# A second pairwise sum on VectorE before the softmax denominators, with new pacing, priorities and end, in an attention and MLP kernel

## The chip, the cores and the metric

The kernel runs on one core of a Trainium2 chip. The metric is the device time of one launch in microseconds (us); lower is better. The profiled span is some 2 us shorter than the measured time of the same execution (1088.9 against 1091.05 us before).

## The reference, cut to what matters

```python
def reference(A_x, A_wqkv, A_wo, B_x, B_w1, B_b1, B_w2, B_b2):
    xn = _layernorm(A_x)                                   # (1, 2048, 1024)
    # A: attention, 32 heads of 32, softmax(q k / sqrt(32)) v, then @ wo
    s = _A_ref(xn, A_wqkv, A_wo)
    # B: layernorm, w1 (1024 -> 3584), tanh gelu, w2 (3584 -> 1024)
    g = _silu(_B_ref(xn, B_w1, B_b1, B_w2, B_b2))
    return A_x + s * g
```

All tensors are bf16. The outputs of the two branches meet only in the last line, so the MLP's dense matmuls can fill TensorE's time between those of attention.

## The kernel before

Attention is cut into 512 units. A unit is one group of four heads (8 groups), one block of 256 queries (8 blocks) and two blocks of 128 keys. For each unit TensorE makes scores (S), ScalarE makes two exponentials of 1024 columns, VectorE adds the two key blocks (PA), and TensorE makes P times V and the denominators, which are PA times a matrix of ones:

```python
def unit(u, pv):                                    # cut
    o = add("PE", s_fn, 2 * Q256, TL, ...)          # scores of the unit
    for h in range(2):
        x = act(... activation(P[pi]..., ACT.Exp, scale=SCALE) ...)
    pa = dve(lambda e: e.tensor_tensor(PA[ai][:], P[pi][:, :, 0, :], P[pi][:, :, 1, :], op=ALU.add), ..., 2.5)
    vc = add("PE", ...)                             # P times V: 8 matmuls
    oc = add("PE", ...)                             # ones times PA: 4 matmuls
    oc.alt = pa                                     # if pa is late, 8 matmuls on P instead
```

A planner in Python lays all operations of all engines into fixed orders before the program is built; on the chip each engine works through its own order and waits on semaphores. The planner lets a score unit go first unless "dense" work (MLP, projections, output items) is behind:

```python
if c[1] == 0 and heads["pro"] >= len(self.queues["pro"]) and \
        state["done"] < dense_total * (state["s"] - dense_slack) / total_units:
    paced = c            # the score unit is taken only if nothing else is ready
...
plan.run(HG * 64, 10)    # dense_slack = 10 units
```

An output item is eight matmuls of 512 columns (one for each head group), a gate multiply from PSUM and an add on VectorE; two items make one stored block of 128 rows. The program divides PSUM into eight banks: six hold scores, and two are shared by the dense items and the open P,V item. An eviction is the copy of a finished result out of a bank; it frees the bank.

The softmax here doesn't subtract the row's maximum and nothing guards it: scores larger than these inputs give would overflow.

Of the kernel before, what the change touches and what calls it, by code (L numbers as in the profile page):

```python
# [11 lines left out]

ENGS = ("PE", "ACT", "DVE", "POOL", "SP")
# [7 lines left out]
class _Item:  # L21
    def __init__(self, kind, due=0):
        self.kind = kind
        self.due = due
        self.chunks = []
        self.evacs = []
        self.bank = None
        self.k = 0


class _Plan:
# [3 lines left out]
    def __init__(self):  # L35
        self.ops = []
        self.last_w = {}
        self.readers = {}
        self.s_queue = []
        self.pv_queue = []  # L40
        self.queues = {"pro": [], "proj": [], "mlp": [], "wo": []}
# [36 lines left out]
    def run(self, total_units, dense_slack):  # L78
# [59 lines left out]
        def pick(e, t):  # L138
            while soon[e] and soon[e][0][0] <= t:
                _, _, o = heapq.heappop(soon[e])  # L140
                if not o.dead:
                    pend[e].append(o)
            best = None
            bk = None
            if e == "SP" and pend[e] and min(o.prio for o in pend[e]) >= 5 and state["bw"] > t + 1500:
                wake(state["bw"] - 1400, e)
                return None
            for o in pend[e]:
                k = (o.prio, o.idx)
                age = t - o.ready  # L150
                if e == "ACT" and o.prio > 0 and age > 2500:
                    k = (-1, o.idx)
                if e == "DVE" and o.prio >= 3 and age > 3500:
                    k = (1.5, o.idx)
                if bk is None or k < bk:
                    best, bk = o, k
            if best is not None and e == "DVE" and best.prio >= 2 and soon[e]:
                r = min((x[0] for x in soon[e] if x[2].prio <= 1), default=INF)
                if r < t + best.occ - 400:
                    wake(r, e)  # L160
                    return None
            if best is not None:
                pend[e].remove(best)
            return best
# [18 lines left out]
        def next_items(t):  # L183

            out = []
            u = state["s"]
            q = self.queues
            pr = q["proj"][heads["proj"]] if heads["proj"] < len(q["proj"]) else None
            if heads["pro"] < len(q["pro"]):
                out.append("pro")  # L190
            if pr is not None and u >= pr.due:
                out.append("proj")
            for n in ("mlp", "wo"):
                if heads[n] < len(q[n]):
                    out.append(n)
            if pr is not None and "proj" not in out and (u >= pr.due - 12):
                out.append("proj")
            return out

        def opens_at(it, r):  # L200

            off = 0.0
            for c in it.chunks:
                if c.left == 0:
                    r = max(r, c.ready - off)
                elif it.kind == "wo":
                    return None
                off += 1.2 * c.occ
            return r

        def pe_step(t):
# [20 lines left out]
            if state["pvopen"] is not None:  # L232
                it = state["pvopen"]
                o = it.chunks[it.k]
                if o.alt is not None and o.alt.start is None and not o.alt.dead and it.exp_of[o.unit].fin is not None \
                        and t > it.exp_of[o.unit].fin + 4000:
                    p = o.alt
                    p.dead = True
                    p.start = p.fin = t
                    if p in pend["DVE"]:  # L240
                        pend["DVE"].remove(p)
                    o.occ *= 2
                    release(p, t)
                if o.left == 0:
                    cands.append((o.ready, 1, o, None))
            if state["dopen"] is not None:
# [4 lines left out]
            else:  # L251
                bf = bank_for(t)
                if bf is not None:
# [49 lines left out]
            if opening is not None:  # L303
# [12 lines left out]
            if cls == 0:  # L316
                state["s"] += 1
            else:
                it = o.item
                it.k += 1  # L320
                if it.k == len(it.chunks):
                    if cls == 1:
                        state["pvopen"] = None
                    else:
# [6 lines left out]

        for o in self.ops:
            if o.left == 0:
# [111 lines left out]
def bass_recurrent_scan__mha_block__mixer_channel_mlp__prompt_kernel(  # L445
# [34 lines left out]
    TRIG = 7  # L480
# [3 lines left out]
    with ExitStack() as st:  # L484
# [163 lines left out]
        load_x(2)  # L648
        load_x(3)
        load_v(0)  # L650
        for t in range(4, NT):
            load_x(t)
# [163 lines left out]
        def w1_item(c, pi):  # L816
# [4 lines left out]
            it = _Item("mlp")  # L821
            for k in range(8):
# [13 lines left out]
                c_b16(512), [("xb", i3)], [("sq", p % 2)], 3)  # L836
            dve(lambda e: e.scalar_tensor_tensor(ut_t[i3][:], sq_t[p % 2][:], 1.0 / GA, xb_t[i3][:], op0=ALU.add, op1=ALU.mult),  # L837
                c_f32(512), [("sq", p % 2), ("xb", i3)], [("ut", i3)], 3)
# [4 lines left out]
                c_f32(512), [("ut", i3), ("xb", i3)], [("h", hs)], 3)  # L843
# [84 lines left out]
        def proj(hg, w):  # L928
# [9 lines left out]
            for k, (kind, t) in enumerate(lst):  # L938
                due = 64 * w + 3 + int(k * (48 if w < 6 else 26) / len(lst))
                if kind == "v":  # L940
                    plan.queues["proj"].append(v_item(hg // 2, t, "proj", due))
                else:
                    plan.queues["proj"].append(qk_item(hg, 0 if kind == "q" else 1, t, wk if kind == "k" else wq, due))

        def unit(u, pv):
# [18 lines left out]
            for h in range(2):  # L964
                x = act(lambda e, h=h: e.activation(P[pi][:, 2 * h:2 * h + 2].rearrange("p j k q -> p (j k q)"),  # L965
                                                    ps[:, pr[h] * 1024:(pr[h] + 1) * 1024], ACT.Exp, scale=SCALE),
                        c_act(1024), [("S", pr[h])], [("P", pi, h)], 0)
            pa = dve(lambda e: e.tensor_tensor(PA[ai][:], P[pi][:, :, 0, :], P[pi][:, :, 1, :], op=ALU.add), c_b16(1024),  # L968
                     [("P", pi, 0), ("P", pi, 1)], [("PA", ai)], 2.5)
# [8 lines left out]
            oc = _Op()  # L978

            def o_fn(e, b):  # L980
                if pa.dead:
                    for kk in range(2):
                        ins = quad(e, lambda j: bankp(b, j, 256, 512), lambda j: ones[:], lambda j: P[pi][:, j, kk, :],
                                   False, False)
                    return ins
                return quad(e, lambda j: bankp(b, j, 256, 512), lambda j: ones[:], lambda j: PA[ai][:, j, :], False, False)
            oc = add("PE", lambda e: o_fn(e, pv.bank), Q256, TL, [("PA", ai), ("P", pi, 0), ("P", pi, 1), ("ones",)], [], item=pv)
            oc.alt = pa
            oc.unit = u
            pv.exp_of[u] = x  # L990
            return x, vc, oc

        def norm(g, pv, ot_dst, W, extra=()):
            i = g % 2
            a = dve(lambda e: e.transpose(nt_t[i][:], bank(pv.bank, 256, 512)), c_ps(256), [], [("nt", i)], 1, pv)
            dve(lambda e: e.tensor_copy(nv_t[i][:], bank(pv.bank, 0, 256)), c_ps(256), [], [("nv", i)], 1, pv)
# [4 lines left out]
                [("nr", i)], [("nb", i)], 2.2)  # L1001
            return dve(lambda e: e.tensor_tensor(ot_dst, nv_t[i][:], nb_t[i][:], op=ALU.mult), c_f32(256),
# [3 lines left out]
        for tq in range(1, 4):  # L1006
            plan.queues["proj"].append(qk_item(0, 0, tq, wq0, 16 * tq - 12))
        for w in range(HG):
# [23 lines left out]
            for qb in range(NQB):  # L1032
# [3 lines left out]
                vcs, ocs, xs = [], [], []  # L1036
                for kp in range(NKP):
                    x, vc, oc = unit(g * 8 + kp, pv)
                    xs.append(x)
                    vcs.append(vc)  # L1040
                    ocs.append(oc)
                pv.chunks = []
                lag = 3
                for k in range(NKP + lag):
                    if k < NKP:
                        pv.chunks.append(vcs[k])
                    if k >= lag:
                        pv.chunks.append(ocs[k - lag])
# [10 lines left out]
                for t2 in range(2):  # L1059
# [10 lines left out]
                    else:  # L1070
# [3 lines left out]
                    dma(f"xr{ri}", lambda e, xr=xr, tb=tb: e.dma_start(xr, x2[tb * 128:(tb + 1) * 128, :]), 262144, [],  # L1074
                        rt + [("xr", ri, 0), ("xr", ri, 1)])
                    dma(f"gr{ri}", lambda e, gr=gr, tb=tb: e.dma_start(gr, g_d[tb * 128:(tb + 1) * 128, :]), 262144,
                        [("g_d", qb, q) for q in range(4)], rt + [("gr", ri, 0), ("gr", ri, 1)])
                    for nh in range(2):
                        it = _Item("wo")
                        for hc in range(HG):  # L1080
                            def fn(e, b, hc=hc, tb=tb, nh=nh):
                                o7 = OTr[:, hc, tb * 128:(tb + 1) * 128] if hc < 7 else ot7[:, tb * 128:(tb + 1) * 128]
                                return full(e, bank(b), o7, wo_sb[hc][:, nh * 512:(nh + 1) * 512], hc == 0, hc == HG - 1)
                            chunk(it, fn, Q512, [("OTr", hc, tb // 4) if hc < 7 else ("OT7", qb), ("wo", hc)])
                        sl_ = slice(nh * 512, (nh + 1) * 512)
                        dve(lambda e, it=it, gr=gr, sl_=sl_: e.scalar_tensor_tensor(gr[:, sl_], bank(it.bank), 0.5, gr[:, sl_],
                                                                                    op0=ALU.mult, op1=ALU.mult),
                            c_ps(512), [], [("gr", ri, nh)], 0, it)
                        dve(lambda e, xr=xr, gr=gr, sl_=sl_: e.tensor_tensor(xr[:, sl_], gr[:, sl_], xr[:, sl_], op=ALU.add),
                            c_b16(512), [("gr", ri, nh)], [("xr", ri, nh)], 1)  # L1090
                        plan.queues["wo"].append(it)
                    dma(f"os{ri}", lambda e, xr=xr, tb=tb: e.dma_start(out2[tb * 128:(tb + 1) * 128, :], xr), 262144,
                        [("xr", ri, 0), ("xr", ri, 1)], rt)

        plan.run(HG * 64, 10)
# [59 lines left out]
```

## Time and profile before

| | before |
|---|---|
| time, median (range) | 1091.28 us (1090.8 to 1092.17), 3 runs |
| profiled span | 1088.9 us |
| busy: TensorE, ScalarE, VectorE | 1044.3, 1032.5, 858.1 us |
| first exponential starts | 17.3 us |
| last exponential ends | 1072.4 us |
| after it, to the end | 16.5 us |

Two engines are busy 95 and 96 per cent of the time, so busy time alone doesn't say which one bounds. The chain that ended last helps: it follows the last instruction back through whatever released each step. This line of the page before gives its shares by engine:

```profile
ACT 64%; PE 31%; DVE 3%; POOL 1%; DMA 1%; issue 0%; POOLq 0%
```

Two thirds of the chain are ScalarE, almost a third is TensorE: the bound changes hands.

### The profile page before, as it was taken

How to read it: one execution, taken by the hardware profiler on the slowest of the kernel's cores; microseconds unless marked ns; L12 is line 12 of the kernel's file. 1: busy time of each engine (PE TensorE's matmuls, PEld its weight loads, DVE VectorE, ACT ScalarE, POOL GpSimd, SP SyncE). 2: the span in 40 equal slices, each digit the busy share in tenths (PEclk: the TensorE clock that was granted, in tenths of full speed). 3: DMA queues.
4: the chain of work that ended last, by engine and by line, in shares of the span. 5: the costliest groups of instructions: out<-in, count | busy, mean ns of one | idle time of the engine just before them, and what ended most of it. 6: DMA issues, size and time to landing. Idle time of an engine off the chain costs nothing.

```text
span 1088.9 us, 34312 instructions
## 1 busy us (share of the span) xinstructions
PE 1044.3 (96%) x15309; PEld 665.7 (61%) x15309; DVE 858.1 (79%) x1633; ACT 1032.5 (95%) x1186; POOL 32.5 (3%) x42
## 2 busy tenths in 40 slices
PE   5898899999999999999999999999999999899998
PEld 4665456566666666556675657656676567565443
DVE  6789677698778967896778877987779787966776
ACT  4799798999999999999999999999999999999993
POOL 4600000000000000000000000000000000000000
PEclk9999899999999999999999999999999999999999
DMA  9345337443464556433464547533365677572442
GB/s 261 98 123 169 95 81 203 115 112 93 133 196 133 148 148 183 135 101 98 132 190 126 141 126 205 162 107 94 96 184 153 179 213 206 164 214 83 130 140 85
DMA packets 285516, 156.62 MB, mean 144 GB/s; under 512 B 23610, under 2 KB 276026, under 8 KB 285370
## 3 DMA queue, kind: packets, MB, share of 16 engines
q1 hardware_dynamic: 285370, 154.44, 49.7%
q8 instruction: 120, 1.97, 0.8%
q14 instruction: 26, 0.21, 0.1%
HBM read 142.35 MB, written 12.06 MB: 142 GB/s over the span
## 4 chain that ended last, share of the span: by engine, by line
ACT 64%; PE 31%; DVE 3%; POOL 1%; DMA 1%; issue 0%; POOLq 0%
ACT P L965 59%; PE ps L612 20%; PE ps L607 6%; PE ps L956 5%; ACT ut L839 4%; ACT gw L871 1%; POOL gw L748 1%; DVE stats L734 0%; DVE PA L968 0%; DMA w1r<-in_B_w_dram 0%; DVE hT L841 0%; POOLq L1105 0%; ACT big L724 0%; DMA hT<-in_A_x_dram 0%; DVE xb L831 0%
## 5 line engine op out<-in xcount | busy, mean ns | idle before, releaser
L965 ACT ACTIVATE P<-ps 128x1024 bf16<-128x1024 f32 x1024 | 979.5, 1170 | 25.2 <-PE ps L956 22.5
L968 DVE TENSOR_TENSOR PA<-P 128x1024 bf16<-128x1024 bf16 x511 | 343.8, 684 | 113.8 <-ACT P L965 61.0
L612 PE MATMUL ps<-yT,w1r 128*128 128x256 bf16 x1792 | 230.2, 273 | 3.7 <-DVE xb L831 2.4
L612 PE MATMUL ps<-w2r,hT 128*128 128x256 bf16 x1792 | 226.7, 274 | 3.8 <-DVE hT L841 2.9
L612 PEld LDWEIGHTS ps<-yT,w1r 128*128 128x128 bf16 x1792 | 162.4, 98 | 59.2 <-issue 28.9
L612 PEld LDWEIGHTS ps<-w2r,hT 128*128 128x128 bf16 x1792 | 163.8, 98 | 54.2 <-issue 28.3
L607 PE MATMUL ps<-P,V 128*32 128x256 bf16 x4096 | 157.9, 273 | 0.3 <-ACT P L965 0.2
L612 PE MATMUL ps<-big,qk 128*128 128x512 bf16 (+1 forms) x552 | 133.6, 372 | 1.7 <-ACT big L724 1.1
L612 PE MATMUL ps<-qk,big 128*128 128x256 bf16 (+1 forms) x736 | 124.7, 306 | 4.7 <-ACT big L724 1.8
L607 PE MATMUL ps<-PA,ones 128*32 128x256 bf16 x2044 | 117.9, 274 | 0.0
L607 PEld LDWEIGHTS ps<-P,V 128*32 128x32 bf16 x4096 | 101.1, 96 | 24.4 <-issue 12.9
L956 PE MATMUL ps<-qk 32*128 32x256 bf16 x2048 | 102.1, 274 | 11.6 <-ACT P L965 10.4
L956 PE MATMUL ps<-QKT 32*128 32x256 bf16 x2048 | 101.7, 273 | 4.3 <-ACT P L965 4.2
L841 DVE SCALAR_TENSOR_TENSOR hT<-ut,xb 128x512 bf16<-128x512 f32 x112 | 76.2, 682 | 24.6 <-ACT ut L839 24.4
L612 PEld LDWEIGHTS ps<-qk,big 128*128 128x128 bf16 x736 | 65.0, 98 | 46.4 <-issue 15.2
L839 ACT ACTIVATE ut<-ut 128x512 f32<-128x512 f32 x112 | 89.0, 805 | 1.0 <-DVE ut L837 1.0
L831 DVE TENSOR_TENSOR xb<-ps,b1T 128x512 bf16<-128x512 f32 x112 | 76.6, 684 | 9.2 <-PE ps L612 8.3
L612 PEld LDWEIGHTS ps<-big,qk 128*128 128x128 bf16 x552 | 49.0, 99 | 54.5 <-issue 16.0
L837 DVE SCALAR_TENSOR_TENSOR ut<-sq,xb 128x512 f32<-128x512 bf16 x112 | 76.7, 687 | 1.5
L956 PEld LDWEIGHTS ps<-qk 32*128 32x128 bf16 x2048 | 30.4, 92 | 76.6 <-ACT P L965 71.0
L956 PEld LDWEIGHTS ps<-QKT 32*128 32x128 bf16 x2048 | 30.3, 92 | 71.0 <-ACT P L965 66.1
L607 PEld LDWEIGHTS ps<-PA,ones 128*32 128x32 bf16 x2044 | 52.4, 96 | 15.7 <-issue 13.9
(62 smaller groups left out, 486.7 us busy)
## 6 DMA issues: line engine op xcount, KB each, us to landing
w1r<-in_B_w_dram SPq DMA_DIRECT2D x112, 512.0 KB, 4.4
w2r<-in_B_w_dram SPq DMA_DIRECT2D x128, 448.0 KB, 4.3
qk<-in_A_wqkv_dram SPq DMA_DIRECT2D x16, 256.0 KB, 3.3
g_scratch<-gw SPq DMA_DIRECT2D x32, 128.0 KB, 3.0
o_scratch<-ot SPq DMA_DIRECT2D x56, 64.0 KB, 2.8
big<-o_scratch SPq DMA_DIRECT2D x28, 128.0 KB, 3.0
hT<-in_A_x_dram SPq DMA_DIRECT2D x10, 256.0 KB, 5.4
qk<-in_A_wqkv_dram SPq DMA_DIRECT2D x4, 512.0 KB, 3.8
```

Of the source, the lines that this page charges most:

```text
L607: ins = e.matmul(dst(j), lhsT=lhsT(j), rhs=rhs(j), start=start, stop=stop, tile_position=(0, 32 * j), skip_group_check=True)
L612: return e.matmul(dst, lhsT=lhsT, rhs=rhs, start=start, stop=stop, skip_group_check=True)
L748: pool(lambda e, t=t: e.tensor_scalar(xnb[t % 4], xst[t], lnp[:, t, 1:2], lnp[:, t, 5:6], op0=ALU.mult, op1=ALU.add), 950, [XS(t), ("nb_", ...
L831: dve(lambda e: e.tensor_tensor(xb_t[i3][:].rearrange("p (k t) -> p k t", k=2), bank(it.bank).rearrange("p (k t) -> p k t", k=2), b1T[:, 2 ...
L837: dve(lambda e: e.scalar_tensor_tensor(ut_t[i3][:], sq_t[p % 2][:], 1.0 / GA, xb_t[i3][:], op0=ALU.add, op1=ALU.mult), c_f32(512), [("sq", ...
L839: act(lambda e: e.activation(ut_t[i3][:], ut_t[i3][:], ACT.Tanh, scale=GC * GA), c_act(512), [("ut", i3)], [("ut", i3)], 1)
L841: dve(lambda e: e.scalar_tensor_tensor(hT[:, hs].rearrange("p k t -> p (k t)"), ut_t[i3][:], 1.0, xb_t[i3][:], op0=ALU.add, op1=ALU.mult), ...
L871: act(lambda e: e.activation(zh_t[zi], z_t[zi], ACT.Tanh, scale=0.5), c_act(512), [("z", zi)], [("zh", zi)], 1)
L956: ins = e.matmul(bank(b0[j], kk * 256, (kk + 1) * 256), lhsT=QKT[sl][32 * j:32 * j + 32, 1, kb * 128:(kb + 1) * 128], rhs=QKT[sl][32 * j:3 ...
L965: x = act(lambda e, h=h: e.activation(P[pi][:, 2 * h:2 * h + 2].rearrange("p j k q -> p (j k q)"), ps[:, pr[h] * 1024:(pr[h] + 1) * 1024], ...
L968: pa = dve(lambda e: e.tensor_tensor(PA[ai][:], P[pi][:, :, 0, :], P[pi][:, :, 1, :], op=ALU.add), c_b16(1024), [("P", pi, 0), ("P", pi, 1 ...
```

## The change

Its intent: take half of the denominators' matmuls off TensorE by one more add on VectorE where VectorE has time, and arrange the rest so that ScalarE is always fed. The core of the diff, with cuts marked:

```diff
+GRACE2 = 1200    +NOPA = 8     +SLACK = 30     +RESERVE = 800   +GLAST = 12
+AGE_A = 1000     +HOLD = 500   +PBPRIO = 3.2   +GRACE1 = 2500   ... (one a line)
 # 1 the second add: one group of ones-matmuls for two units
+        def ones_pair(u, pv, pas, xs):
+            pb = dve(lambda e: e.tensor_tensor(PA[a0][:], PA[a0][:], PA[a1][:], op=ALU.add), c_b16(1024),
+                     [("PA", a1)], [("PA", a0)], PBPRIO)
+            ...  # given up when late: PA of each unit, or P itself
+            for v, pa in ((u, pas[0]), (u + 1, pas[1])):
+                if v < NOPA or v >= HG * 64 - 2:
+                    plan.skip.append(pa)
+            if u < NOPA or u >= HG * 64 - 4:
+                plan.skip.append(pb)
 # 2 pacing
-        plan.run(HG * 64, 10)
+        plan.run(HG * 64, SLACK)
 # 3 priorities: overdue limits, VectorE's hold, a bank kept for the next P,V item
-                if e == "ACT" and o.prio > 0 and age > 2500:
+                if e == "ACT" and o.prio > 0 and age > AGE_A:
-                if r < t + best.occ - 400:
+                if r < t + best.occ - HOLD:
+                if bf is not None and RESERVE and state["pvopen"] is None and ...:
+                    if x.start is not None and x.fin < t + RESERVE:
+                        bf = None
+            gp = 2.05 if pi >= GLAST else 3
 # 4 projections by place among the MLP items
-                due = 64 * w + 3 + int(k * (48 if w < 6 else 26) / len(lst))
+                due = 64 * w + HARD + int(k * 14 / len(lst))
+                plan.queues["proj"][-1].after = lo + int(k * n / len(lst))
 # 5 start: six instead of four blocks of x before the V weights
-        load_x(2); load_x(3); load_v(0)
+        for t in range(2, 6): load_x(t)
+        load_v(0)
 # 6 end: the last four output items do 7 of 8 contractions in banks that the scores
 #   have left, the 8th when the last head group is there; halved stores; two adds on
 #   GpSimd; one copy less in the last normalisation
+                        if lastq:
+                            itb = _Item("wo"); itb.host = it; plan.wob.append(itb)
 ...
```

## The prediction

> **What bounds the kernel now.** I read the page first (busy time, costliest groups), then the windows view cut where the two busy engines change, then the timeline of ScalarE and TensorE where ScalarE idles, then the timeline of the end. The page alone does not decide, because two engines are nearly full:
>
> ```profile
> PE 1044.3 (96%) x15309; PEld 665.7 (61%) x15309; DVE 858.1 (79%) x1633; ACT 1032.5 (95%) x1186; POOL 32.5 (3%) x42
> ...
> L965 ACT ACTIVATE P<-ps 128x1024 bf16<-128x1024 f32 x1024 | 979.5, 1170 | 25.2 <-PE ps L956 22.5
> L968 DVE TENSOR_TENSOR PA<-P 128x1024 bf16<-128x1024 bf16 x511 | 343.8, 684 | 113.8 <-ACT P L965 61.0
> ...
> L607 PE MATMUL ps<-PA,ones 128*32 128x256 bf16 x2044 | 117.9, 274 | 0.0
> ```
>
> L965 is the exponential of the scores, L968 the sum of the two key blocks of a unit, and L607 on PA,ones the softmax denominators: 511 units of four matmuls. The means overlap (matmul ends are modelled, activations are pipelined), so I take work from distances between starts. The ScalarE timeline gives them:
>
> ```profile
> 301.12 5.78 ACT L965 ACTIVATE P<-ps 128x1024 bf16<-128x1024 f32 x6
> 306.54 0.87 ACT L839 ACTIVATE ut<-ut 128x512 f32<-128x512 f32 x1
> 307.06 3.10 ACT L965 ACTIVATE P<-ps 128x1024 bf16<-128x1024 f32 x3
> ```
>
> Six exponentials take 306.54 - 301.12 = 5.42 us, 0.904 us each; a tanh takes 0.52 us. ScalarE's work is then 1024 x 0.904 + 144 x 0.52 (112 tanh of the MLP, 32 of the gate) + 16 x 0.904 (copies of the transposes) = 926 + 75 + 14 = 1015 us. The last exponential ends at 1072.4 us, so ScalarE stood still some 57 us before it. Windows tell where (the columns are stretch, length, then busy time and instruction count of PE, PEld, DVE, ACT and POOL, then clock and DMA):
>
> ```profile
> 0.00:17.30 17.30, 7.00 (x51) 5.03 (x52) 8.71 (x25) 3.53 (x4) 7.50 (x14) 1.00 0.96 303
> 17.30:50.00 32.70, 27.18 (x311) 21.12 (x311) 27.12 (x69) 25.02 (x27) 25.00 (x28) 1.00 0.50 128
> 50.00:100.00 50.00, 47.01 (x719) 31.86 (x716) 44.42 (x87) 47.08 (x55) 0.00 (x0) 1.00 0.46 129
> 100.00:150.00 50.00, 43.93 (x614) 24.04 (x614) 35.49 (x68) 43.37 (x51) 0.00 (x0) 0.93 0.34 95
> 150.00:200.00 50.00, 49.82 (x666) 33.90 (x664) 37.04 (x67) 44.86 (x53) 0.00 (x0) 1.00 0.64 177
> 200.00:600.00 400.00, 395.07 (x6023) 257.30 (x6016) 324.04 (x606) 399.68 (x463) 0.00 (x0) 1.00 0.48 135
> 600.00:950.00 350.00, 341.34 (x5108) 223.76 (x5107) 282.90 (x529) 347.98 (x405) 0.00 (x0) 1.00 0.55 156
> 950.00:1072.40 122.40, 120.92 (x1764) 63.44 (x1761) 88.29 (x169) 120.98 (x134) 0.00 (x0) 1.00 0.46 139
> 1072.40:1088.90 16.50, 11.98 (x75) 5.26 (x73) 10.06 (x20) 0.03 (x1) 0.00 (x0) 0.95 0.23 79
> ```
>
> ScalarE's idle time is 13.8 us before the first exponential, 7.7 to 50 us, 2.9 + 6.6 + 5.1 = 14.6 from 50 to 200, and only 3.7 in the 872 us after that. (Distances between starts above the ordinary ones add some 12 us of small slips there, below what busy time shows.) So from 200 us on ScalarE is the bound, and TensorE keeps step beside it; the start and the last 16.5 us are not ScalarE's.
>
> **Why ScalarE idles early.** In the TensorE timeline at 163 us, 36 MLP matmuls run without a score unit between them, while ScalarE's row shows the matching gap:
>
> ```profile
> 163.67 4.10 PE L612 MATMUL ps<-w2r,hT 128*128 128x256 bf16 x36
> 167.71 0.40 PE L956 MATMUL ps<-qk 32*128 32x256 bf16 x8
> ```
>
> ```profile
> 168.16 2.85 ACT L965 ACTIVATE P<-ps 128x1024 bf16<-128x1024 f32 x3 [4.66 <-PE ps L956]
> ```
>
> This is the program's pacing: a score unit yields when dense work is more than 10 units behind. It is a choice of order, not a lack of data. The end is a row of output items: eight matmuls, L1086, L1089, again every 1.73 us from 1074.7 to 1086.4 us, then a store that ends 2.5 us after its issue.
>
> **What the Trainium skill says.** "TensorE: Matmul & The Clock Gate", section "Wait — 56ns, not 53.3ns?": warm matmuls follow each other every N / 2.4 GHz plus about 2.5 ns, so 109 ns for 256 columns and 216 for 512. The trace agrees: eight 512-column matmuls take 1.73 us in the last items. "TensorEngine Tiling (Array Packing)", section "Key Properties": tiles work in parallel, and a change of tiling mode drains the array. The trace agrees: a group of four PA,ones matmuls advances by 0.11 us (131.51 to the next at 131.62), and a score unit costs 0.33 us to the next start instead of 2 x 0.109. "VectorE: DVE Perf Modes", section "The perf-mode tier table (the rule you actually need)": an add of two bf16 tiles in SBUF runs at two elements a cycle, so 1024 elements need 533 ns at its 0.96 GHz plus a fixed part. The trace has adds 0.60 us apart in back-to-back runs (record 0.684).
>
> **The change part by part.**
>
> *Second add.* Two PA tiles are added on VectorE and one group of four ones-matmuls serves two units. At most 256 groups go; the first four pairs and the last two are excluded and use P or PA directly. A pair's add is also given up when the TensorE plan reaches it over 1.2 us after its exponentials; the last pair of each query block has its exponentials just before its denominators are wanted, so I expect most of those 64 to fall back. Kept: 190 to 240, say 210. TensorE saves 210 x 0.11 = 23 us, less (8 units without the first add cost one more group each) 1 us. VectorE gains 210 x 0.60 = 126 us less about 6 us for the ten first adds dropped: 858 + 0.684 x 200 = 995 us as the page counts it, some 93% of a shorter span.
>
> TensorE's work now, from distances: scores 512 x 0.42 (0.22 plus two mode changes of some 0.1) = 215; P,V 112; ones 56; MLP 3584 x 0.109 = 391; 512-column projections and output 728 x 0.216 = 157; 256-column projections 592 x 0.109 = 65; the rest 12: 1008 us. It falls to about 986, below ScalarE's 1015. In the stretch after 200 us, where ScalarE has no hole to fill, this saving is worth next to nothing: I count 3 us for fewer slips. It is what lets the other parts work.
>
> *Pacing slack 10 to 30, projections by MLP position, other priorities.* Score units may run 30 units ahead. The paced gaps from 50 to 200 us should go: of 14.6 us I keep 4. Spreading projections among MLP items only pays if VectorE's evictions had been late; the page's waits of TensorE on VectorE are few, so zero.
>
> *Start.* No first adds on VectorE for eight units, and the load order x before V. At 37.6 us four L968 adds stood between normalisation and eviction work. I count 3 of the 7.7 us. The first exponential itself hangs on the same loads: nothing.
>
> *End.* The last four output items do seven of eight contractions in banks that the scores have left, and wait for the last head group only with the eighth; the stores are halved, one add goes to GpSimd. After the last exponential remain: P,V and up to six ones-groups 0.9 us, transpose, reciprocal, transpose, multiply (the nt to qk rows at 1073.58 to 1076.3 took 2.7, now one copy less) 2.2, last matmuls and item order 1.5, eviction 0.7, add 0.4, store 2.5: 8.2 us, call it 8.5. It was 16.5: 8 us gained.
>
> Sum: 3 + 10.6 + 3 + 8 = 24.6 us. Of the early and middle part, 16.6 us, I give back 20 per cent (3.3 us) for new waits on VectorE and imperfect order: 21.3 us, 1091.3 - 21.3 = 1070. That counts only 3 of the 12 us of small slips; they come where a score unit waits for TensorE to finish something else, and TensorE now has some 30 us to spare against ScalarE, so I let it take three quarters of them, 6 us more: 1064.
>
> **The rivals.** *TensorE is the bound:* the page has it at 96%, and nearly all slices are full. Then the 22 us come off in full with the early and end gains, 1091 - 22 - 10 - 8 = 1051. Against it stands ScalarE's 747.7 of 750 us busy from 200 to 950. *VectorE becomes the bound:* at 93% it holds PSUM banks longer before evictions, and TensorE then waits. For it: the early windows show DVE at 44.4 of 50 us just where ScalarE also idles. Against: second adds have the lowest priority and are dropped when late. It would give 1075 to 1090. *The larger slack moves work to the end:* 20 more units of backlog are 20/512 of about 590 us of dense work (391 + 157 + 42), 23 us, and the end would grow instead of shrink: about 1080. Against: TensorE has some 30 us less work than ScalarE and can catch up.
>
> **Range and chances.** 1064 is between the ScalarE-bound sum and its better case; the TensorE rival gives the low side 1050, the two losing rivals the high side, cut at 1079. Faster by 2% means below 1069.5: 1064 has 5.5 us to spare, against a half-range of some 14, so 0.67. Slower by 2% would need a badly laid order: 0.02. Within 2%: 0.31.
>
> **What would show it.** Right: ones-matmuls fall from 2044 to about 1200; L965 still 0.904 us apart and ScalarE full after 200 us; the window 50 to 200 us has under 6 us of ScalarE idle; the last exponential ends near 1052; 8 to 9 us follow it. Wrong: ScalarE idles in the middle behind TensorE waits on VectorE evictions; more than four output items after the last exponential; ScalarE's early gaps are still there, only moved; or second adds mostly dropped, with ones-matmuls above 1600.

## The result

| | before | after |
|---|---|---|
| time, median (range) | 1091.34 us (1090.8 to 1092.17), 4 runs | 1066.8 us (1066.05 to 1067.25), 4 runs |
| profiled span | 1088.9 | 1065.3 |
| last exponential ends | 1072.4 | 1051.2 |
| after it, to the end | 16.5 | 14.1 |
| ones-matmuls (on PA + on P) | 2044 + 8 | 1280 + 80 |
| second adds | 0 | 182 |

The ratio is 0.9774 (95% interval 0.9757 to 0.9791): 2.3 per cent faster. Ratios here and below are the mean time of one kernel's runs over that of the other's runs of the same rounds, so they are not quite the ratio of the medians quoted. Executions over 1.5% slower than the fastest of the same kernel are left out of the means.

The busy times and the groups concerned, from the page after (columns as in the prediction; L1016 is the exponential, L1022 the first add, L1039 the second, L655 the ones-matmuls):

```profile
PE 1022.9 (96%) x14561; PEld 645.8 (61%) x14617; DVE 947.5 (89%) x1803; ACT 1029.6 (97%) x1186; POOL 33.0 (3%) x44
...
L1016 ACT ACTIVATE P<-ps 128x1024 bf16<-128x1024 f32 x1024 | 984.0, 1211 | 10.6 <-PE ps L1007 7.6
L1022 DVE TENSOR_TENSOR PA<-P 128x1024 bf16<-128x1024 bf16 x502 | 337.4, 682 | 62.9 <-PE ps L655 36.1
...
L1039 DVE TENSOR_TENSOR PA<-PA 128x1024 bf16<-128x1024 bf16 x182 | 123.3, 681 | 1.0
...
L655 PE MATMUL ps<-PA,ones 128*32 128x256 bf16 x1280 | 71.5, 275 | 0.0
```

The exponentials' idle time went from 25.2 to 10.6 us, VectorE gained 89 us of busy time, and TensorE lost 513 - 340 = 173 groups of four ones-matmuls (513 = 2052 / 4, 340 = 1360 / 4), some 19 us at 0.11 us each. The chain of the page after:

```profile
ACT 89%; PE 7%; DVE 2%; POOL 1%; DMA 0%; issue 0%
```

ScalarE now makes up nine tenths of what led to the end. The windows view of after, cut at the same times up to 950 us and then at about the last exponential (stretch, length, busy time and count of PE, PEld, DVE, ACT, POOL, then clock and DMA):

```profile
0.00:17.30 17.30, 6.73 (x45) 4.46 (x46) 10.16 (x31) 3.65 (x5) 7.81 (x15) 1.00 0.92 281
17.30:50.00 32.70, 29.85 (x352) 23.48 (x349) 21.29 (x57) 27.71 (x30) 22.91 (x28) 1.00 0.56 150
50.00:100.00 50.00, 45.23 (x721) 28.54 (x715) 43.65 (x86) 48.50 (x57) 0.00 (x0) 0.97 0.40 114
100.00:150.00 50.00, 48.12 (x719) 27.17 (x713) 47.26 (x90) 50.00 (x59) 0.00 (x0) 1.00 0.32 89
150.00:200.00 50.00, 49.98 (x730) 34.57 (x728) 44.27 (x84) 50.00 (x59) 0.00 (x0) 1.00 0.71 196
200.00:600.00 400.00, 394.90 (x5670) 252.82 (x5691) 369.70 (x690) 399.94 (x465) 0.00 (x0) 1.00 0.48 137
600.00:950.00 350.00, 340.52 (x4967) 222.73 (x4981) 318.63 (x594) 348.57 (x407) 0.00 (x0) 1.00 0.59 168
950.00:1051.50 101.50, 97.36 (x1327) 47.21 (x1332) 85.32 (x165) 101.24 (x112) 0.00 (x0) 1.00 0.38 119
```

ScalarE's idle time is the length less its busy time. From 17 to 50 us it went from 7.7 to 5.0, from 50 to 200 us from 14.7 to 1.5. That is 15.9 of the 21.2 us by which the last exponential ends earlier. Most of the rest are the small slips that busy time doesn't show: summed over the trace, the distances between ScalarE's starts above the ordinary ones (0.904 and 0.52 us) come to 15.8 us after 200 us before, and to 11.6 us after.

The end is where the prediction expected most and got little. TensorE's timeline after the last exponential of after (start, duration, engine, line, operation, operands, count):

```profile
1052.88 0.38 PE L660 MATMUL ps<-qk 128*128 128x512 bf16 x1
1053.10 1.67 PE L660 MATMUL ps<-qk,big 128*128 128x512 bf16 x7
1054.61 0.38 PE L660 MATMUL ps<-qk 128*128 128x512 bf16 x1
...
1060.01 1.67 PE L660 MATMUL ps<-qk,big 128*128 128x512 bf16 x7
1061.52 0.38 PE L660 MATMUL ps<-qk 128*128 128x512 bf16 x1
```

Output items still follow each other every 1.73 us. In all 42 output matmuls start after the last exponential (49 before), and the split items stand in the same row as whole ones. A row of VectorE's timeline, the multiply of the last normalisation, shows why the split has little to give:

```profile
1054.23 0.41 DVE L1077 TENSOR_TENSOR qk<-ps,nb 128x256 bf16<-128x256 f32 x1
```

The last head group is ready at 1054.6 us, before the first of the four last items has started its first seven contractions (1054.83). TensorE's backlog sets the end, not the wait for that head group.

### The profile page after: what moved, and what is told of

The parts are those of the page before. It is cut to its first block, busy times and chain, and to the rows that moved or that the text cites. A ratio compares the mean times of both kernels' runs of the same rounds, so it can differ in the third digit from the quotient of the medians.

```text
span 1065.3 us, 32988 instructions
## 1 busy us (share of the span) xinstructions
PE 1022.9 (96%) x14561; PEld 645.8 (61%) x14617; DVE 947.5 (89%) x1803; ACT 1029.6 (97%) x1186; POOL 33.0 (3%) x44
## 4 chain that ended last, share of the span: by engine, by line
ACT 89%; PE 7%; DVE 2%; POOL 1%; DMA 0%; issue 0%
ACT P L1016 82%; ACT ut L888 5%; PE ps L660 4%; ACT gw L920 1%; PE ps L655 1%; DVE stats L782 1%; PE ps L1007 1%; POOL gw L796 1%; POOL lnp L810 0%; DMA hT<-in_A_x_dram 0%; DVE V L732 0%; DVE qk L760 0%; DVE mv L784 0%; DVE yT L860 0%; PE ps L769 0%
## 5 line engine op out<-in xcount | busy, mean ns | idle before, releaser
L1016 ACT ACTIVATE P<-ps 128x1024 bf16<-128x1024 f32 x1024 | 984.0, 1211 | 10.6 <-PE ps L1007 7.6
L1022 DVE TENSOR_TENSOR PA<-P 128x1024 bf16<-128x1024 bf16 x502 | 337.4, 682 | 62.9 <-PE ps L655 36.1
L660 PE MATMUL ps<-w2r,hT 128*128 128x256 bf16 x1792 | 229.4, 274 | 1.8 <-DVE hT L890 1.3
L660 PEld LDWEIGHTS ps<-w2r,hT 128*128 128x128 bf16 x1792 | 161.4, 98 | 55.1 <-issue 33.4
L655 PE MATMUL ps<-P,V 128*32 128x256 bf16 x4096 | 147.5, 276 | 1.6 <-DVE xb L880 0.7
L660 PE MATMUL ps<-big,qk 128*128 128x512 bf16 (+1 forms) x509 | 122.4, 368 | 6.1 <-ACT big L772 2.3
L1039 DVE TENSOR_TENSOR PA<-PA 128x1024 bf16<-128x1024 bf16 x182 | 123.3, 681 | 1.0
L660 PE MATMUL ps<-qk,big 128*128 128x256 bf16 (+1 forms) x723 | 121.7, 305 | 2.5 <-issue 1.6
L655 PEld LDWEIGHTS ps<-P,V 128*32 128x32 bf16 x4096 | 101.6, 97 | 26.6 <-issue 13.1
L1007 PE MATMUL ps<-qk 32*128 32x256 bf16 x2048 | 102.1, 274 | 9.8 <-ACT P L1016 8.4
L1007 PE MATMUL ps<-QKT 32*128 32x256 bf16 x2048 | 101.8, 273 | 5.5 <-ACT P L1016 4.8
L888 ACT ACTIVATE ut<-ut 128x512 f32<-128x512 f32 x112 | 92.1, 835 | 0.0
L1007 PEld LDWEIGHTS ps<-qk 32*128 32x128 bf16 x2048 | 30.4, 92 | 75.9 <-ACT P L1016 72.9
L1007 PEld LDWEIGHTS ps<-QKT 32*128 32x128 bf16 x2048 | 30.4, 92 | 75.0 <-ACT P L1016 73.5
L655 PE MATMUL ps<-PA,ones 128*32 128x256 bf16 x1280 | 71.5, 275 | 0.0
```

The source lines that it names most:

```text
L655: ins = e.matmul(dst(j), lhsT=lhsT(j), rhs=rhs(j), start=start, stop=stop, tile_position=(0, 32 * j), skip_group_check=True)
L660: return e.matmul(dst, lhsT=lhsT, rhs=rhs, start=start, stop=stop, skip_group_check=True)
L888: act(lambda e: e.activation(ut_t[i3][:], ut_t[i3][:], ACT.Tanh, scale=GC * GA), c_act(512), [("ut", i3)], [("ut", i3)], 1)
L1007: ins = e.matmul(bank(b0[j], kk * 256, (kk + 1) * 256), lhsT=QKT[sl][32 * j:32 * j + 32, 1, kb * 128:(kb + 1) * 128], rhs=QKT[sl][32 * j:3 ...
L1016: x = act(lambda e, h=h: e.activation(P[pi][:, 2 * h:2 * h + 2].rearrange("p j k q -> p (j k q)"), ps[:, pr[h] * 1024:(pr[h] + 1) * 1024], ...
L1039: pb = dve(lambda e: e.tensor_tensor(PA[a0][:], PA[a0][:], PA[a1][:], op=ALU.add), c_b16(1024), [("PA", a1)], [("PA", a0)], PBPRIO)
```

## The experiments

My theory (A): ScalarE bounds from some 50 us on as long as TensorE's order feeds it; the slack lets scores go first, which puts dense work off; TensorE's saved matmuls pay that debt; what isn't paid stands as output items after the last exponential. Rivals: (B) TensorE is the bound all along, and its saving comes off in full whatever else is done; (C) ScalarE hides the saving, and the slack alone does the work; (D) VectorE's added load delays evictions.

The numbers of all runs. Idle is ScalarE's from 50 to 200 us, by windows. "Items left" are output matmuls that start after the last exponential, divided by eight. The base of every ratio is the kernel before. Runs (in part from another chip) are compared by these ratios; their intervals are about 0.0015 to 0.002 wide on each side, so a difference under some 0.0025 is not resolved. A difference to the changed kernel in us is the difference of the two ratios times 1091.3 us. All runs but one (early_out, not in the table) gave the correct result. A slip is the time by which the distance between two starts of ScalarE exceeds the ordinary one, as above.

| run | ratio to before | median us | idle 50 to 200 | last exp. ends | then | items left |
|---|---|---|---|---|---|---|
| before | 1 | 1091.3 | 14.7 | 1072.4 | 16.5 | 6.1 |
| changed | 0.9774 | 1066.8 | 1.5 | 1051.2 | 14.1 | 5.3 |
| no_add2 | 0.9888 | 1079.1 | 2.6 | 1055.9 | 21.1 | 9.3 |
| slack10 | 0.9934 | 1083.5 | 12.0 | 1067.6 | 14.0 | 5.3 |
| old_prio | 0.9929 | 1083.3 | 6.9 | 1061.6 | 20.5 | 8.9 |
| old_proj | 0.9808 | 1070.4 | 1.2 | 1051.1 | 17.3 | 7 |
| old_start | 0.9807 | 1070.1 | 1.9 | 1054.5 | 14.1 | 5.3 |
| old_end | 0.9798 | 1068.2 | 2.2 | 1050.6 | 15.3 | 5.9 |
| add_alone | 1.0074 | 1098.1 | 17.1 | 1080.5 | 15.3 | 5.9 |
| slack20_alone | 1.0011 | 1092.1 | 3.0 | 1066.3 | 25.6 | 11.8 |
| add_slack | 0.9988 | 1090.0 | 4.5 | 1067.5 | 20.0 | 7.9 |
| x_first8 | 0.9762 | 1065.2 | 2.3 | 1049.9 | 14.1 | 5.3 |

### The add taken out: no_add and no_add2

```diff
-            if u < NOPA or u >= HG * 64 - 4:
+            if True:
                 plan.skip.append(pb)
```

> The changed kernel with every second add left out: each pair of units again uses two groups of four ones-matmuls (182 groups come back, 182 x 0.109 = 20 us of TensorE), all else as changed. Theory A (ScalarE bounds, the add only gives TensorE room to catch up after the early lead of the scores): ScalarE stays as full from 50 to 900 us, the loss shows as more output items after the last exponential and small slips, 1072 to 1079 us. Rival B (TensorE bounds all along): the whole 20 us come back, about 1086 us. Rival C (the add is worth nothing because ScalarE hides it): within 2 us of 1067.

Measured: ratio 0.9896 (0.9879 to 0.9912) over three runs, 1078.19 to 1080.15 us. The profiled execution fell at a clock of 0.754 and took 1284.5 us; its trace is not used. The same kernel again for a trace:

> The same kernel as the run without second adds, whose profile fell on an execution at a clock of 0.754; this one is for a trace at full clock. Time 1078 to 1081 again. If the add only gives TensorE room: ScalarE as full as in the changed kernel up to 600 us (idle time from 50 to 600 us under 3 us), and the loss split between more ScalarE slips after 600 us and a tail longer than 14 us by 5 us or more (some 10 output items instead of 6). If ScalarE idles early instead, the room theory is wrong.

Measured: 0.9888, 1078.95 and 1079.2 us. Without the add the kernel is 12.4 us slower than with it (13.3 by the first run): neither 20 (B) nor nothing (C), and at or just over the upper end of what theory A expected (1072 to 1079 us). The windows before and after the last exponential:

```profile
950.00:1055.90 105.90, 103.34 (x1514) 54.33 (x1516) 74.53 (x142) 104.90 (x117) 0.00 (x0) 1.00 0.43 128
1055.90:1077.00 21.10, 17.58 (x107) 8.08 (x108) 12.02 (x24) 0.01 (x1) 2.31 (x2) 1.00 0.38 125
```

ScalarE is nearly as full as in the changed kernel, and its last exponential ends only 4.7 us later. The other 7.0 us stand after it: 74 output matmuls instead of 42, and 32 x 0.216 = 6.9 us. This is theory A's debt, countable. Two expectations inside it missed: ScalarE's idle time from 50 to 600 us is 2.6 + 1.1 = 3.7 us and not under 3, and its slips after 600 us grew by only 1.2 us (5.0 + 3.1 against 5.6 + 1.3 in the two stretches 600 to 950 and after), those from 200 to 600 us by 1.8.

### The slack taken back: slack10

```diff
-SLACK = 30
+SLACK = 10
```

> The changed kernel with the pacing slack back at 10 units. Theory A (the slack removed the early paced gaps of ScalarE): 8 to 13 us of ScalarE idle time return between 50 and 200 us, 1074 to 1080 us, and the tail after the last exponential is no longer than 14 us. Rival (with 19 us less TensorE work the dense work is never 10 units behind, so the slack is idle): within 2 us of 1067. Rival (the slack costs at the end what it gives at the start): under 1067, with a tail of 10 us or less.

Measured: 0.9934 (0.9918 to 0.9951), 17.5 us slower than the changed kernel. Its windows:

```profile
50.00:100.00 50.00, 45.94 (x708) 31.15 (x710) 45.52 (x90) 43.38 (x51) 0.00 (x0) 1.00 0.45 128
100.00:150.00 50.00, 45.91 (x632) 26.27 (x636) 42.58 (x81) 44.62 (x52) 0.00 (x0) 1.00 0.35 94
150.00:200.00 50.00, 49.22 (x714) 33.25 (x713) 44.45 (x83) 50.00 (x61) 0.00 (x0) 1.00 0.71 198
```

6.6 and 5.4 us of ScalarE idle time are back in the first two stretches, 12.0 to 200 us against 1.5, as expected; the tail is unchanged (14.0). The time was expected at 1074 to 1080 us and is 1083.5, because another 5 us or so came back later (slips of 8.2 and 3.9 us from 600 to 950 and after it, against 5.6 and 1.3). So the pacing alone brings early gaps back, at a clock of 1.00 in these rows. (In the kernel before, 2.7 of the 14.7 us lie in or within 3.4 us after a stretch of half clock from 121.4 to 128.2 us, which followed waits of TensorE; the rest has no such neighbour.) The program also shows that 30 means "never": laid with a slack of 24, 30, 42 or a million, which needs no chip, it is the same program, so in the changed kernel no score unit is held back.

### Each alone on the kernel before, and both together

Slack 20 alone (24 and 30 can't be laid out on the kernel before: the planner gets stuck):

```diff
-        plan.run(HG * 64, 10)
+        plan.run(HG * 64, 20)
```

> The kernel before with one number changed, the pacing slack 20 in place of 10 (30 alone can't be laid out: the projections of the next head group then come too late for the planner). Without the second add TensorE has 1008 us of work against ScalarE's 1015. If the slack pays by itself: 1080 to 1085, the early gaps at least halved and the tail after the last exponential still 16 us. If the early lead has to be paid for later, because TensorE has nothing to spare: 1088 to 1095, with less ScalarE idle time before 200 us and more after it or a longer tail.

Measured: 1.0011 (0.9998 to 1.0025), no gain, the second alternative. Idle from 50 to 200 us fell from 14.7 to 3.0 us and the last exponential ended 6.1 us earlier. The window after that:

```profile
1066.30:1092.00 25.70, 21.78 (x118) 9.78 (x120) 15.93 (x32) 0.03 (x1) 0.00 (x0) 1.00 0.39 133
```

25.6 us follow instead of 16.5, with 94 output matmuls instead of 49: 45 x 0.216 = 9.7 us of debt. Of the 11.7 us of idle time that went, 5.6 came back as slips after 200 us (21.4 against 15.8), and the debt at the end took more than the rest, so rival C falls. (The profiled execution, 1094.11 us, was the slowest of the four.)

The second add alone: the changed file with slack 10 and the old start, projection times, priorities and end. The new order of P,V and ones-matmuls within an item, and the planner's wait of output items for their loads, stay in; what they do by themselves was not run.

```diff
-SLACK = 30
+SLACK = 10
 ... and parts 3 to 6 of the diff undone (NOPA = 0, RESERVE = 0, AGE_A = 2500, HOLD = 400, GRACE1 = 4000, ...)
```

> The kernel before with the second add alone: slack 10, old load order, old projection times, old priorities, old end. Theory A (ScalarE bounds): the early gaps shrink only as far as TensorE gets ahead, the tail stays at 14 to 17 us: 1080 to 1087. Rival B (TensorE bounds): the 19 us come off in full, about 1072. Rival (VectorE holds evictions up): 1090 or more.

Measured: 1.0074 (1.0057 to 1.009), **slower** than the kernel before although 166 second adds were made and TensorE had 164 groups less. B falls here: a saving of some 18 us on TensorE came with a loss of 8. Theory A's own forecast, 1080 to 1087, missed as well; the time lies where rival D had put it, at 1090 or more. Its windows:

```profile
100.00:150.00 50.00, 41.53 (x507) 22.38 (x509) 40.44 (x74) 40.35 (x47) 0.00 (x0) 0.90 0.34 95
...
600.00:950.00 350.00, 334.04 (x4922) 216.52 (x4939) 305.84 (x570) 344.68 (x399) 0.00 (x0) 0.99 0.53 150
```

ScalarE idles 9.7 us in the first of these (6.6 before) and 5.3 in the second (2.0 before), and TensorE is less busy too (334.0 of 350 us against 341.3): both engines wait, and the clock in the first is 0.90 (0.93 before). So the saved time can be lost on the way; the table in the section on the priorities shows where.

Both together, still with the old parts 3 to 6:

```diff
 ... as in the run above, but
+SLACK = 30
```

> The kernel before with the second add and the slack of 30 together; old load order, projection times, priorities and end. Each alone gained nothing (add alone 1.0074, slack 20 alone 1.0011 of before). If they need each other (the slack fills ScalarE early, the add pays TensorE's debt): 1078 to 1086, early gaps gone as in the changed kernel. If their effects only add up: 1092 or more.

Measured: 0.9988 (0.9973 to 1.0003). The early gaps went (idle 4.5 us), but it missed both forecasts, 1078 to 1086 if the two need each other and 1092 or more if they only add up: the add and the slack don't suffice as a pair. 7.9 output items stand after the last exponential, and ScalarE slips 10.7 us from 600 to 950 us (5.6 in the changed kernel). Something among parts 3 to 6 had to be worth some 23 us, and my prediction had booked 11 for them, none of it for the priorities.

### The priorities put back: old_prio

```diff
-AGE_A = 1000        +AGE_A = 2500
-HOLD = 500          +HOLD = 400
-RESERVE = 800       +RESERVE = 0
-GLAST = 12          +GLAST = 99
-GRACE1 = 2500       +GRACE1 = 4000
```

> The changed kernel with the old priorities: no bank held ready for the next P,V item, ScalarE's overdue limit 2500 instead of 1000 ns, VectorE's hold 400 instead of 500 ns, no raised rank for the late MLP columns, drop limit of first adds 4000 ns. The prediction gave these nothing. If nothing: within 3 us of 1067. If the priorities are what keeps TensorE's order dense under a VectorE at 89%: 1074 to 1084, with a longer tail.

Measured: 0.9929 (0.9909 to 0.9949), 16.9 us slower than the changed kernel. This is the largest surprise: a part that removes no operation from any engine. The waits of TensorE and ScalarE in this run (waiting engine and line, what it waited for: us in total, times, longest):

```profile
PE ps L660 <- DVE hT L890: 6.9, 9, 1.7
PE ps L655 <- DVE xb L880: 3.9, 4, 2.0
...
ACT P L1016 <- PE ps L1007: 10.6, 8, 4.5
...
ACT P L1016 <- PE ps L655: 7.8, 11, 2.4
```

and the same waits in the changed kernel:

```profile
PE ps L660 <- DVE hT L890: 1.3, 2, 0.7
PE ps L655 <- DVE xb L880: 0.7, 1, 0.7
...
ACT P L1016 <- PE ps L1007: 7.6, 3, 5.0
ACT P L1016 <- PE ps L655: 2.9, 3, 1.4
```

Two things grew. In the two lines shown TensorE waits 8.8 us more for VectorE's MLP results (hT is the activation that the second MLP matmul reads, xb the eviction that frees a bank): that is rival D. And exponentials wait 4.9 us more for P,V and ones-matmuls (L655), which free the buffers that an exponential writes, and 3.0 more for scores (L1007). In the end ScalarE finishes 10.4 us later, and 8.9 instead of 5.3 items are left.

A third thing grew with them. The mean clock is 0.990 to 0.991 in old_prio, add_alone and add_slack, against 0.996 and 0.997 in the two kernels. Their traces show stretches of 3.4 or 6.8 us in which TensorE is granted half its clock. Here are the 3.4 us before and after the start of one in old_prio (windows as above, the clock third from the end):

```profile
100.40:103.80 3.40, 1.38 (x27) 0.66 (x28) 2.75 (x5) 2.65 (x5) 0.00 (x0) 1.00 0.73 214
103.80:107.20 3.40, 3.40 (x76) 2.75 (x68) 3.18 (x6) 1.76 (x2) 0.00 (x0) 0.50 0.33 93
```

The whole, up to the last exponential, in us (waits of TensorE on VectorE are all such lines of the waits view, over the whole span):

| run | TensorE waits on VectorE | at half clock | ScalarE idle then and 3.4 us after |
|---|---|---|---|
| before | 10.0 | 6.8 | 2.7 |
| changed | 5.5 | 6.8 | 2.5 |
| old_prio | 15.7 | 20.5 | 7.7 |
| add_alone | 20.6 | 20.5 | 9.4 |
| add_slack | 17.6 | 20.5 | 7.3 |

In these five runs every such stretch began after 3.4 us in which TensorE had been busy for less than 1.9 us. It is no threshold: 1.36 us of 3.4 from 363.7 us in add_alone had no such sequel. At half clock matmuls take about twice as long: in the kernel before, ten of 256 columns took 2.25 us to the score unit behind them (122.41 to 124.66 us), against 1.19 us for ten at full clock (317.02 to 318.21). So 13.7 us more at half clock cost TensorE 6.8 us of full-clock work, on top of the waits that came first. How much of the 16.9 us is the wait and how much the clock no run separates. Nor was it run apart on the chip which of the five numbers does how much; two of them, ScalarE's overdue limit and the bank kept for P,V, are not rules for VectorE. Both questions stay open.

### Projections, start and end put back

```diff
 old_proj
-                due = 64 * w + HARD + int(k * 14 / len(lst))
+                due = 64 * w + 3 + int(k * (48 if w < 6 else 26) / len(lst))
-                plan.queues["proj"][-1].after = lo + int(k * n / len(lst))
+                plan.queues["proj"][-1].after = 10 ** 6
 ...              (and the old rule for taking a projection early)
 old_start
-NOPA = 8
+NOPA = 0
-        for t in range(2, 6): ...
+        for t in range(2, 4): ...
 old_end
-                    lastq = qb == NQB - 1
+                    lastq = False
-            last = g == HG * NQB - 1
+            last = False            (and the score banks are not given out)
```

> The changed kernel with the projections due at the old times (by score unit) instead of at places among the MLP items. The prediction gave this part zero. If it is zero: within 3 us of 1067. If laying them by VectorE load is what keeps evictions in time with VectorE at 89%: 1072 or more, with TensorE waits on VectorE copies and less ScalarE load after 200 us.

Measured: 0.9808 (0.9795 to 0.9822), some 3.7 us slower. ScalarE is as full as in the changed kernel, and 7 items instead of 5.3 are left at the end. 20 second adds fewer were made (162), which would fit projections that crowd VectorE, but what cost the time wasn't tested further. It is not the zero that was predicted, and not 5 us either, so neither of the two forecasts holds; the expected VectorE waits didn't show in ScalarE's load.

> The changed kernel with the old load order (V weights after four blocks of x) and with first adds on VectorE for the first eight units too. The changed trace has 2.7 us less ScalarE idle time between 17 and 50 us and about 1.5 us less at 50 to 100. If that is this part's work: 1069 to 1072. If it was the slack's: within 1.5 us of 1067.

Measured: 0.9807 (0.9793 to 0.982), some 3.6 us slower. ScalarE's idle time from 17 to 50 us is 7.7 us again, as in the kernel before, and the last exponential ends 3.3 us later with the same 14.1 us after it. The whole effect is in the first 50 us and travels through the kernel undiminished: here, where ScalarE bounds, an early gap closed is worth its full length. The two halves of this part (load order, no first adds) were not run apart.

> The changed kernel with the end of the kernel before: no split of the last four output items, no use of the score banks, whole stores, the copy before the last normalisation, adds on VectorE. The trace of the changed kernel shows six output items back to back on TensorE after the last exponential, the last normalisation done long before the first of the split items needs it. If TensorE sets the end: 0 to 2 us longer, 1067 to 1069. If the end part gave the 8 us of the prediction by another way: about 1075.

Measured: 0.9798 (0.9783 to 0.9812), 2.6 us by ratios, at the edge of what is resolved. The trace agrees with about one: 15.3 us after the last exponential instead of 14.1, 47 matmuls instead of 42. (One of its four executions took 1070.91 us, at a mean clock of 0.993; the other three average 1068.0.) The prediction's 8 us aren't there.

### A different end, and one step further at the start

Since work for TensorE stood at the end, I tried to do the first seven contractions of the last eight items earlier, gate them, add them to x, and leave only the eighth contraction (in pseudocode, not the lines of the edit):

```diff
+ early = qb >= NQB - 2
+ tmp = ps * 0.5 * g ; x += tmp        (after 7 contractions, any time)
+ g = ps * 0.5 * g ; x += g            (after the 8th)
```

> The changed kernel with a different end: the first seven contractions of the eight output items of the last two query blocks are done, gated and added to x while ScalarE still works, and only the eighth contraction waits for the last head group (eight more gate multiplies and adds on VectorE). The tail of the changed kernel is 14.1 us with six items of 1.73 us on TensorE in a row. If TensorE sets that tail, it falls to about 10 us: 1062 to 1064. If the last normalisation, evictions and the store set it: within 1 us of 1067. If the extra VectorE work delays the score sums: above 1067.

Measured: ratio 0.983, and a **wrong result** (relative error 0.24): in my edit a Python closure read the flag `early` after the loop had ended, so the eighth matmul of every output item overwrote the sum. Number, shape and order of the instructions don't depend on that, so I still read its timing, with that caution. It failed as an improvement too. Of the 56 early matmuls (eight items of seven) 31 were still undone when the last P,V item was through, because TensorE had no room before; and the VectorE work now came in one block at the very end (19.0 us after the last exponential). The window of that stretch:

```profile
1055.00:1074.00 19.00, 9.97 (x73) 4.59 (x72) 14.88 (x30) 0.03 (x1) 2.26 (x2) 0.88 0.16 56
```

TensorE is busy for 10.0 of 19 us and VectorE for 14.9. The trace of another order of these items was not taken.

The start gave 3.6 us, so I went a step further in its direction:

```diff
-        for t in range(2, 6):
+        for t in range(2, 8):
```

> The changed kernel with eight instead of six blocks of x loaded before the V weights: further in the direction that was worth part of 3 us in the run with the old start. If the first 50 us still wait for x blocks: 0.5 to 1.5 us under the changed kernel, 1065.3 to 1066.3, ratio about 0.9765. If the V weights are now what is late: above 1067.

Measured: 0.9762 (0.9748 to 0.9777), 1065.22 us, about as expected. ScalarE idles 3.9 us from 17 to 50 us (5.0), the last exponential ends 1.3 us earlier, and the span is 1.3 us shorter. It is the fastest kernel and clearly beats the one before. Against the changed kernel its interval overlaps, and there is one trace of each, so that it is the better of the two is likely but not shown.

## Why the prediction was right

The time was predicted as 1064 and is 1066.8; faster by over 2 per cent had 0.67. It came out right, but several terms of its sum were wrong in opposite directions, and that they partly cancel is luck. By its steps:

**ScalarE is the bound after 200 us: right.** Its busy time is 399.94 of 400 and 348.57 of 350 us in the changed kernel, and its share of the chain that ended last rose from 64 to 89 per cent. The early gap closed in the start part arrived at the end in full.

**Early gaps are the pacing's: right.** Expected 10.6 of 14.6 us, got 13.2 of 14.7 in the changed kernel, and slack10 brought 10.5 of it back. What the prediction passed over is the 0.93 in the clock column of its own row from 100 to 150 us: not every early gap was a choice of order alone.

**Start 3 us: right.** 2.7 us of idle time from 17 to 50 us; the run with the old start lost 3.6 in time.

**Second adds "190 to 240, say 210", ones-matmuls "about 1200": slightly over.** 182 adds were kept, and 1280 + 80 matmuls are left. VectorE rose to 947.5 us, not 995.

**The add is worth 3 us in place, and "lets the other parts work": first half wrong, second half right.** Taking it out of the changed kernel costs 12.4 us, and 6.9 us of output matmuls more are left at the end. The step that failed is that where ScalarE "has no hole to fill, this saving is worth next to nothing": it overlooked that the slack's debt of dense work must be done by the end, so TensorE's total counts although it isn't the bound in the middle. For the same reason its rival of the larger slack (work moved to the end) is real: slack20_alone has just that, and without the add or the priorities 9.3 and 8.9 items are left in place of the changed kernel's 5.3.

**End 8 us: a term mis-sized.** The tail shrank by 2.4 us, from 16.5 to 14.1. What failed is the prediction's list of what remains after the last exponential: it has 1.5 us for "last matmuls and item order", and no backlog of dense work. 5.3 items of 1.73 us were left, 9.2 us. The sign "more than four output items after the last exponential" had been named as one that would show the prediction wrong, and it came.

**Priorities nothing, projections zero: wrong.** The projections' part is worth some 3.7 us, the priorities' 16.9 in the run without them. Neither removes an operation. With the old priorities TensorE waits 15.7 us on VectorE instead of 5.5 and runs 20.5 us at half clock instead of 6.8; that the waits bring the loss about fits this, but no run shows it apart. The prediction gave the projections zero because the page's waits of TensorE on VectorE are few, which were those of a VectorE at 79 per cent, not 89. Its rival "VectorE becomes the bound" it dismissed because second adds come last and are dropped when late; add_alone, with that rule in force, lost 8 us and has 20.6 us of such waits.

**The sum.** The losses of the runs that undo one part are 12.4 + 17.5 + 16.9 + 3.7 + 3.6 + 2.6 = 56.7 us, over twice the 24.7 us gained (0.0226 x 1091.3). On the kernel before, the add alone is worth -8 us, a slack of 20 alone -1, and add and slack 30 together 1. The parts are not a sum; each needs the others. The prediction's total was near because it summed places in time rather than parts: up to the last exponential it had 16.6 - 3.3 + 6 = 19.3 us, and the spans show 21.2; after it 8, and they show 2.4. That the small slips shrink was right, with 4.2 us of them gone after 200 us where 9 were booked (3 and 6). Which part of the change filled which gap was the weak side of it.

## What to carry to other kernels

Where two engines are both nearly full, ask not which one is the bound but where the one's debt is paid: letting the first run ahead only moves the second's work to the end, unless that work has shrunk. An operation moved to a third engine is worth its time only if what that engine owes the others still comes when it is wanted, so a change of load and a change of priorities have to be judged, and undone, together. Count what is left after the bounding engine's last instruction, in items and microseconds: here that told where the time went in no_add2, slack20_alone and old_prio, but not in slack10 or add_alone, which lost theirs earlier. And look at the clock in the windows: short waits of TensorE came before every stretch of half clock listed here.

## What the Trainium skill lacked or had wrong

- "ScalarE: Activation LUTs", section "What ACT_TABLE_LOAD costs": it gives 186 ns plus 0.833 ns a column for an activation with immediate operands, and an overlap of about 93 ns between successive ones, so 1039 - 93 = 946 ns for 1024 columns. A lone exponential took 1.03 us here as stated, but in a row they start 0.904 us apart, an overlap of some 0.13 us; over 1024 of them the difference is 43 us.
- "TensorEngine Tiling (Array Packing)", section "Key Properties": it says that a change of tiling mode drains the array, without a cost. Here a score unit of eight row-tiled matmuls among full ones took 0.33 us to the next start (300.18 to 300.51 us in the kernel before) and delayed its own by about 0.1 us, against 2 x 0.109 = 0.22 us for the eight, four at a time: an estimate of about 0.1 us for each change.
- "TensorE: Matmul & The Clock Gate": neither it nor another page says how busy, short of standing idle, TensorE must be over a stretch for its clock to stay whole. In the five traces of the table above, half clock followed 3.4 us in which TensorE was busy for 0.4 to 1.9 us and waited for at most 2.0 us in one piece.
